# An attention stage's hand-written order: denominators ahead, all score blocks ahead of transposes, the next pair's preparation among the groups

## The chip, the cores and the metric

The kernel runs on one core of one Trainium2 chip. The metric is the device time of one execution in microseconds (us), and the time shown is a median of several executions. Work runs on five engines side by side, each of which takes its own instructions strictly in order: TensorE (PE: matmuls and transposes; its weight loads are listed as PEld), VectorE (DVE), ScalarE (ACT), GpSimd (POOL) and SyncE (SP, which here issues all DMAs). An instruction that waits for another engine holds up everything that stands behind it on its own engine.

## What is computed

Attention over 4 batches x 8 heads, 576 positions, head size 64, with a causal mask, mixed with a linear-attention memory; its output feeds two feed-forward blocks.

```python
scores = scale * np.matmul(q, k.transpose(0, 1, 3, 2))    # causal mask, softmax
local = np.matmul(a, v)
q_p = phi(q)                                              # elu(q) + 1
mem_out = einsum('bhsd,bhde->bhse', q_p, M_prev) / (einsum('bhsd,bhd->bhs', q_p, z_prev) + 1e-06)
out = g * mem_out + (1 - g) * local                       # g: one gate per head
...
h = x @ w_in;  x = (h * np.tanh(softplus(h))) @ w_out     # 2304 x 512, width 2048
x = (((x @ w1) * (x @ w2)) @ w3) @ w_out2                 # width 1024
```

## The kernel before

The attention stage takes two heads at a time: 16 pairs, each with all 576 positions. Function `pair(p)` writes out one pair's work, and it is software-pipelined over two pairs: `now` is pair p, whose scores are computed, `old` is pair q = p - 1, whose second half is finished, and `new` is pair p + 1, whose inputs are prepared. Pairs 1 to 15 are emitted under `tc.manual_schedule()`, so the order in which `pair` writes the steps sets the order on the engines; pair 0 and the trailing call for pair 15's rest are placed by a scheduler.

The steps, with the names that the rows below use:

- `s_blocks(p, e, blocks)`: scores of head e (0 or 1) of the pair for the row blocks given (block 3 is 128x512, block 2 128x384, blocks 1 and 0 share a bank), two matmuls each from `eqk` (head 0) or `oqk` (head 1) and `lk`,`qz` into a `psA` bank (three banks); then on DVE the masked negative maximum (L405, with a short read of the accumulator), then on ACT the exponential with its row sum (L410). `s_last(p)` does the same for the last 64 rows of both heads (`s4`, matmuls on `qd`).
- `inverted` (L391, L392) takes the reciprocal of the row sums, `normed` (L400) scales a block by it.
- `pt_g(p, i)`: transposes of one group of scaled blocks on PE into a `psF` bank (two banks), and one copy out on ACT (L470). Groups 0 to 2 are head 0, 3 to 5 head 1, 6 and 7 the last rows.
- `prep_q`, `prep_k`: PE transposes the raw q and k of the next pair into `psX` banks (three); ACT copies them out (`qt` L319, `hk` L330), POOL or DVE makes the low halves (`hl`, `lk`). `stack` then copies them by DMA into `eqk`, `oqk` and `qz`.
- `prep_phi(p)`: phi of the queries (ACT L366, POOL L367, DVE L368).
- `weigh_phi(q)`: the memory's denominators. PE multiplies phi by z (`zt`, five products of two columns, L59), DVE adds 1e-6 and inverts (`dn`, L380, L381), ACT spreads the ten values over 640 columns (`spread`, L384), PE transposes that (five transposes, L301), DVE multiplies phi by it (L387).
- `pv_main(q)`, `pv_last(q)`: one product of phi and the memory and the products of weights and values, in one `psX` bank; ACT copies out the high half (`xt`, L474), DVE makes the low half (L65).
- `background` is a generator that decodes weights for the next stage in single steps, seven for each weight tile: a 512 KB DMA into `draw` (L92, one buffer), DVE L99, L101, L103, L106, L108, L110, then POOL L111. `pair` takes seven of its steps in each of pairs 2 to 9, and the generator is empty after that.

After the attention stage come the two feed-forward blocks, which are a scheduler's work and are not touched.

Of the kernel before, what the change touches and what calls it, by code (L numbers as in the profile page):

```python
# [14 lines left out]
ALU = mybir.AluOpType  # L15
# [6 lines left out]
def fused_kernel(ctx: ExitStack, tc, q, k, v, M_prev, z_prev, beta, w_in, w_out, w1, w2, w3, w_out2, out):  # L22
    nc = tc.nc
# [271 lines left out]
    def trans(src, evac):  # L295
        for c0, c1 in ((0, 256), (256, S)):
            pt = psX()

            for i in range(2) if c0 == 0 else (2, 3, 4):
                x = min(128 * i, S - 128) - c0  # L300
                nc.tensor.transpose(pt[:, x:x + 128], src[:, i].rearrange("p h d -> p (h d)"), ident)  # L301
            evac(slice(c0, c1), pt[:, 0:c1 - c0])
# [65 lines left out]
        nc.vector.scalar_tensor_tensor(out=t, in0=t, scalar=1.0, in1=r, op0=ALU.min, op1=ALU.add)  # L368
        st[p]["phi"] = t

    def weigh_phi(p):
        b, c = divmod(p, NP)
        t = st[p]["phi"]

        o = psF()[:, 0:2 * NB]
        for i in range(NB):
            x = min(128 * i, S - 128)
            mm(o[:, 2 * i:2 * i + 2], t[:, x:x + 128], zt[b % 2][:, c], True, True)
        dn = ap_.tile([128, 2 * NB], F32, tag="dn", name="dn", bufs=2)
        nc.vector.tensor_scalar(out=dn, in0=o, scalar1=1e-6, scalar2=None, op0=ALU.add)  # L380
        nc.vector.reciprocal(out=dn, in_=dn)  # L381

        w = ap_.tile([128, NB, 2, D], F32, tag="spread", name="spread", bufs=1)
        nc.scalar.copy(  # L384
            out=w.rearrange("p i e d -> p (i e) d"), in_=dn[:, :, None].to_broadcast([128, 2 * NB, D]),
        )
        trans(w, lambda cs, o: nc.vector.tensor_tensor(out=t[:, cs], in0=o, in1=t[:, cs], op=ALU.mult))  # L387

    def inverted(p, e):
        rv = st[p]["sum"][:, slice(8, 9) if e is None else slice(e, 8, 2)]  # L390
        nc.vector.tensor_scalar(out=rv, in0=rv, scalar1=1e-9, scalar2=None, op0=ALU.add)  # L391
        nc.vector.reciprocal(out=rv, in_=rv)  # L392

    def normed(p, ib, e):

        d = st[p]
        og = ogp[:, p % NP]
        s = s4[:, 0:S] if ib == 4 else d["s"][ib, e]
        x = 8 if ib == 4 else 2 * ib + e
        nc.vector.tensor_scalar(  # L400
            out=s, in0=s, scalar1=d["sum"][:, x:x + 1], scalar2=og[:, x:x + 1], op0=ALU.mult, op1=ALU.mult
        )
# [58 lines left out]
    def pt_g(p, gi):  # L461
        d = st[p]
        n = 128 * len(GROUPS[gi])
        t = ap_.tile([128, n], F32, tag=f"pt{gi}", name="pt", bufs=1)
        o = psF()
        for x, (ib, e, jb) in enumerate(GROUPS[gi]):
            src = d["s"][4] if e is None else d["s"][ib, e]
            nc.tensor.transpose(o[:, 128 * x:128 * x + 128], src[:, 128 * jb:128 * jb + 128], ident)  # L468
            d["t"][ib, e, jb] = t[:, 128 * x:128 * x + 128] if e is None else (t, 128 * x)
        nc.scalar.copy(out=t, in_=o[:, 0:n])  # L470
# [82 lines left out]
    def pair(p):  # L553

        now, old, new = p < NPAIR, p > 0, p + 1 < NPAIR
        q = p - 1
        background = first if 2 <= p < 12 else iter(())
        if old:
            ensure_x(q // NP)
        if now and old:  # L560
            stack(p, 1)

        if old:
            inverted(q, 1)
            normed(q, 3, 1)
        if now:
            s_blocks(p, 0, (3,))
        if old:
            normed(q, 2, 1)
        if now:  # L570
            s_blocks(p, 0, (2,))
        if old:
            pt_g(q, 5)
            normed(q, 1, 1)
            normed(q, 0, 1)
        if now:
            s_blocks(p, 0, (0, 1))
        if old:
            pt_g(q, 4)
            pt_g(q, 3)  # L580
            inverted(q, None)
            normed(q, 4, None)
        if new:
            prep_q(p + 1)
        if old:
            pt_g(q, 6)
        if new:
            prep_k(p + 1)
        if old:
            pt_g(q, 7)  # L590
            weigh_phi(q)
        steps(background, 2)

        if now:
            if new:
                stack(p + 1, 0)
                last_q(p + 1)
            inverted(p, 0)
            normed(p, 3, 0)
            s_blocks(p, 1, (3,))  # L600
            normed(p, 2, 0)
            s_blocks(p, 1, (2,))
            normed(p, 1, 0)
            normed(p, 0, 0)
        if old:
            if not now:
                steps(lq0, 100)
                emit_h((0, 0, 0))
            pv_main(q)
        if now:  # L610
            s_blocks(p, 1, (0, 1))
            pt_g(p, 2)
            pt_g(p, 1)
            steps(background, 2)
            pt_g(p, 0)
        if old:
            pv_last(q)
        if now:
            s_last(p)
        steps(background, 2)  # L620
        if new:
            prep_phi(p + 1)
        if p + 2 < NPAIR:
            load_pair(p + 2)
        steps(background, 1)

    lq0 = first
    for p in range(NPAIR + 1):
# [219 lines left out]
```

## Time and profile before

| | |
|---|---|
| median of 2 runs | 1185.32 us (1185.30 and 1185.33) |
| profiled execution | 1186.9 us, of which the span from first to last instruction 1185.1 us |
| busy: PE, PEld | 1063.3 us (90%), 954.0 us (80%) |
| busy: DVE, ACT, POOL | 676.2 us (57%), 551.6 us (47%), 303.9 us (26%) |
| mean granted TensorE clock | 0.949 of full speed |

The profile was taken in one execution. Its own time lies 1.6 us above the median, and 1.8 us of it are outside the span. The busy shares are means over stages that have different limits: up to about 392 us the program is in the attention stage, where PE is busy between 60% and 80% of the time, and after that in matrix products that keep PE nearly full.

### The profile page before, as it was taken

Reading aid. Unit: us, or ns where it says so; the run is one execution under the profiler, and the core shown is the slowest. Engines: PE = TensorE matmul, PEld = TensorE weight load, DVE = VectorE, ACT = ScalarE, POOL = GpSimd, SP = SyncE. Lnnn points to the kernel's source line nnn. Section 1 sums busy time; section 2 is a strip of 40 time slices with the busy share of each in tenths; the row PEclk is TensorE's granted clock in tenths of the full one; section 3 lists DMA queues with packets and bytes.
Section 4 is the critical chain, followed back from the end, with each engine's and each line's share of the span. In section 5 each row is a group of like instructions: output and inputs, shape, how many; then the busy total and the mean of one; then the engine's idle time right before and its main releaser. Section 6 shows DMA issues by size and latency. Waiting matters only on the chain.

```text
span 1185.1 us, 19371 instructions
## 1 busy us (share of the span) xinstructions
PE 1063.3 (90%) x7288; PEld 954.0 (80%) x7288; DVE 676.2 (57%) x1643; ACT 551.6 (47%) x1159; POOL 303.9 (26%) x271
## 2 busy tenths in 40 slices
PE   6777677777778999999999999999999799999998
PEld 5646555555557899999999998999899599999997
DVE  5566756665555798898878875465564122222120
ACT  5545544555553765666655665455232122222221
POOL 5332352233110364555554450010110000000000
PEclk9888988888989999999999999999999899999999
DMA  6555555645522133333442237334121400000000
GB/s 154 122 133 135 123 130 125 135 91 119 126 56 72 55 116 116 125 92 123 132 133 91 90 129 280 125 125 142 61 68 51 169 28 18 18 11 9 19 19 36
DMA packets 111214, 115.68 MB, mean 98 GB/s; under 512 B 73616, under 2 KB 73616, under 8 KB 111120
## 3 DMA queue, kind: packets, MB, share of 16 engines
q1 hardware_dynamic: 111120, 114.44, 34.1%
q8 instruction: 58, 0.95, 0.3%
q14 instruction: 36, 0.29, 0.1%
HBM read 70.79 MB, written 21.50 MB: 78 GB/s over the span
## 4 chain that ended last, share of the span: by engine, by line
PE 55%; DVE 22%; ACT 7%; DMA 5%; POOL 5%; issue 4%; SPq 0%; DVEq 0%; POOLq 0%; ACTq 0%
PE psA L59 25%; PE psX L59 19%; PE psF L59 6%; DVE de L110 3%; ACT s L410 3%; DVE da L106 3%; PE psX L301 2%; DVE de L108 2%; DVE s L405 2%; DVE da L99 2%; PE psF L468 2%; ACT pt L470 2%; POOL da L139 2%; DVE da L101 2%; DVE da L103 2%
## 5 line engine op out<-in xcount | busy, mean ns | idle before, releaser
L111 POOL TENSOR_TENSOR da<-da,de 128x512 f32<-128x512 f32 x72 | 98.7, 1373 | 490.3 <-DVE de L110 388.1
L59 PE MATMUL psX<-gh,wqt 128*128 128x288 f32 x1024 | 210.7, 299 | 12.7 <-DVE x L669 7.0
L59 PE MATMUL psA<-x2h,w12t 128*128 128x256 f32 x1152 | 210.6, 283 | 0.2 <-ACT x2h L764 0.2
L59 PEld LDWEIGHTS psA<-x2h,w12t 128*128 128x128 f32 x1152 | 180.9, 192 | 1.8 <-ACT x2h L764 0.6
L59 PEld LDWEIGHTS psX<-gh,wqt 128*128 128x128 f32 x1024 | 164.9, 189 | 17.7 <-DVE x L669 9.4
L59 PE MATMUL psA<-x2l,w12t 128*128 128x256 f32 x576 | 163.2, 284 | 0.4 <-DVE x2l L65 0.4
L59 PE MATMUL psX<-gl,wqt 128*128 128x288 f32 x512 | 151.3, 296 | 1.1 <-DVE gl L65 1.1
L410 ACT ACTIVATE s<-s,acc 128x128 f32<-128x128 f32 (+3 forms) x144 | 83.5, 580 | 113.5 <-DVE acc L405 112.7
L778 DVE TENSOR_TENSOR bs<-bs,psA 128x256 f32<-128x256 f32 x72 | 30.3, 420 | 167.9 <-PE psA L59 167.7
L468 PE MATMUL psF<-ident,s 128*128 128x128 f32 x400 | 67.6, 291 | 60.7 <-ACT pt L470 37.2
L59 PE MATMUL psA<-xt,wqt 128*128 128x288 f32 x840 | 120.2, 296 | 1.3 <-DVE y L533 1.3
L59 PEld LDWEIGHTS psA<-xt,wqt 128*128 128x128 f32 x840 | 114.5, 188 | 2.0 <-DVE y L533 1.6
L59 PEld LDWEIGHTS psA<-x2l,w12t 128*128 128x128 f32 x576 | 110.5, 192 | 1.3 <-DVE x2l L65 0.7
L59 PE MATMUL psX<-wft,pbuf 128*128 128x512 f32 x432 | 102.2, 396 | 7.5 <-DMA wft<-w_dram 7.5
L468 PEld LDWEIGHTS psF<-ident,s 128*128 128x128 f32 x400 | 46.6, 147 | 76.8 <-ACT pt L470 46.4
L59 PEld LDWEIGHTS psX<-wft,pbuf 128*128 128x128 f32 x432 | 81.9, 191 | 25.4 <-DMA wft<-w_dram 8.7
L59 PEld LDWEIGHTS psX<-gl,wqt 128*128 128x128 f32 x512 | 96.8, 189 | 1.6 <-DVE gl L65 1.3
L779 ACT CAST pbuf<-bs 128x256 fp32r<-128x256 f32 x72 | 29.2, 406 | 109.0 <-DVE bs L778 95.5
L59 PE MATMUL psF<-xt,wqt 128*128 128x288 f32 x552 | 77.7, 295 | 0.4 <-DVE dn L380 0.3
L59 PEld LDWEIGHTS psF<-xt,wqt 128*128 128x128 f32 x552 | 74.5, 188 | 0.8 <-DVE dn L380 0.5
L99 DVE TENSOR_SCALAR da<-draw 128x512 int32<-128x512 int32 x72 | 40.7, 566 | 60.1 <-DMA draw<-in_moe_w_dram 16.2
L536 ACT CAST gh<-y 128x576 fp32r<-128x576 f32 x64 | 43.1, 674 | 66.9 <-DVE y L533 51.1
(117 smaller groups left out, 1959.4 us busy)
## 6 DMA issues: line engine op xcount, KB each, us to landing
draw<-in_moe_w_dram SPq DMA_DIRECT2D x32, 512.0 KB, 3.7
draw<-in_moe_w_out_dram SPq DMA_DIRECT2D x24, 512.0 KB, 3.6
draw<-in_moe_w_in_dram SPq DMA_DIRECT2D x16, 512.0 KB, 4.1
w12t<-w_dram SPq DMA_DIRECT2D x8, 1024.0 KB, 7.3
w_dram<-de SPq DMA_DIRECT2D x24, 256.0 KB, 2.1
w_dram<-da SPq DMA_DIRECT2D x24, 256.0 KB, 2.1
out_dram<-ob SPq DMA_DIRECT2D x18, 256.0 KB, 2.0
eqk<-hk SPq DMA_DIRECT2D x30, 144.0 KB, 2.5
```

Source lines behind the costliest of these rows:

```text
L59: nc.tensor.matmul(o, lhsT=l, rhs=r, start=start, stop=stop)
L99: V.tensor_scalar(out=ai, in0=hw, scalar1=0x7FFFFFFF, scalar2=None, op0=ALU.bitwise_and)
L101: V.tensor_scalar(out=a, in0=a, scalar1=2.0 ** -15, scalar2=122879.9921875, op0=ALU.max, op1=ALU.min)
L103: V.tensor_scalar(out=ai, in0=ai, scalar1=3, scalar2=0x3FFFFFF8, op0=ALU.logical_shift_left, op1=ALU.bitwise_and)
L106: V.scalar_tensor_tensor(out=ai, in0=hw, scalar=-0x40000000, in1=ai, op0=ALU.bitwise_and, op1=ALU.bitwise_or)
L110: V.scalar_tensor_tensor(out=e, in0=lw.bitcast(U32), scalar=2.0 ** -52, in1=e, op0=ALU.mult, op1=ALU.mult)
L111: nc.gpsimd.tensor_tensor(out=a, in0=a, in1=e, op=ALU.add)
L410: nc.scalar.activation(out=s, in_=s, func=AF.Exp, scale=-1.0, bias=a, accum_out=r)
L468: nc.tensor.transpose(o[:, 128 * x:128 * x + 128], src[:, 128 * jb:128 * jb + 128], ident)
L536: nc.scalar.copy(out=gh, in_=y[i])
L778: nc.vector.tensor_tensor(out=bs, in0=bs, in1=pa, op=ALU.mult)
L779: nc.scalar.copy(out=t[:, 0, m], in_=bs)
```

## The change

It touches the order in `pair`, and cuts `weigh_phi` into three steps that can stand apart: `norm_phi` (the products with z, the addition and the reciprocal on DVE), `spread_phi` (the copy on ACT) and `weigh_phi` (the transposes and the multiplication). No instruction is added or removed; each has the same operands and sizes as before.

- `norm_phi(q)` now stands first in a pair, ahead of the first score block.
- All three score steps of head 0 stand ahead of group 5's transposes, with `spread_phi` between block 2 and blocks 0 and 1. All three of head 1 stand ahead of `pv_main`.
- `prep_q` stands before group 5, `prep_k` before groups 4 and 3, and `weigh_phi` between group 3 and group 6.
- `pt_g(p, 0)` moves behind `pv_last`, and the last steps of `background` are taken together (2 + 2 + 3 in place of 2 + 2 + 2 + 1).

```diff
--- before.py
+++ after.py
@@ -368,7 +368,7 @@
         nc.vector.scalar_tensor_tensor(out=t, in0=t, scalar=1.0, in1=r, op0=ALU.min, op1=ALU.add)
         st[p]["phi"] = t
 
-    def weigh_phi(p):
+    def norm_phi(p):
         b, c = divmod(p, NP)
         t = st[p]["phi"]
 
@@ -379,12 +379,19 @@
         dn = ap_.tile([128, 2 * NB], F32, tag="dn", name="dn", bufs=2)
         nc.vector.tensor_scalar(out=dn, in0=o, scalar1=1e-6, scalar2=None, op0=ALU.add)
         nc.vector.reciprocal(out=dn, in_=dn)
-
+        st[p]["dn"] = dn
+
+    def spread_phi(p):
         w = ap_.tile([128, NB, 2, D], F32, tag="spread", name="spread", bufs=1)
         nc.scalar.copy(
-            out=w.rearrange("p i e d -> p (i e) d"), in_=dn[:, :, None].to_broadcast([128, 2 * NB, D]),
+            out=w.rearrange("p i e d -> p (i e) d"),
+            in_=st[p]["dn"][:, :, None].to_broadcast([128, 2 * NB, D]),
         )
-        trans(w, lambda cs, o: nc.vector.tensor_tensor(out=t[:, cs], in0=o, in1=t[:, cs], op=ALU.mult))
+        st[p]["w"] = w
+
+    def weigh_phi(p):
+        t = st[p]["phi"]
+        trans(st[p]["w"], lambda cs, o: nc.vector.tensor_tensor(out=t[:, cs], in0=o, in1=t[:, cs], op=ALU.mult))
 
     def inverted(p, e):
         rv = st[p]["sum"][:, slice(8, 9) if e is None else slice(e, 8, 2)]
@@ -561,6 +568,7 @@
             stack(p, 1)
 
         if old:
+            norm_phi(q)
             inverted(q, 1)
             normed(q, 3, 1)
         if now:
@@ -570,25 +578,26 @@
         if now:
             s_blocks(p, 0, (2,))
         if old:
-            pt_g(q, 5)
-            normed(q, 1, 1)
-            normed(q, 0, 1)
+            spread_phi(q)
         if now:
             s_blocks(p, 0, (0, 1))
         if old:
-            pt_g(q, 4)
-            pt_g(q, 3)
+            normed(q, 1, 1)
+            normed(q, 0, 1)
+        if new:
+            prep_q(p + 1)
+        if old:
+            pt_g(q, 5)
             inverted(q, None)
             normed(q, 4, None)
         if new:
-            prep_q(p + 1)
-        if old:
-            pt_g(q, 6)
-        if new:
             prep_k(p + 1)
         if old:
+            pt_g(q, 4)
+            pt_g(q, 3)
+            weigh_phi(q)
+            pt_g(q, 6)
             pt_g(q, 7)
-            weigh_phi(q)
         steps(background, 2)
 
         if now:
@@ -601,6 +610,7 @@
             normed(p, 2, 0)
             s_blocks(p, 1, (2,))
             normed(p, 1, 0)
+            s_blocks(p, 1, (0, 1))
             normed(p, 0, 0)
         if old:
             if not now:
@@ -608,21 +618,19 @@
                 emit_h((0, 0, 0))
             pv_main(q)
         if now:
-            s_blocks(p, 1, (0, 1))
             pt_g(p, 2)
             pt_g(p, 1)
             steps(background, 2)
-            pt_g(p, 0)
         if old:
             pv_last(q)
         if now:
+            pt_g(p, 0)
             s_last(p)
-        steps(background, 2)
         if new:
             prep_phi(p + 1)
         if p + 2 < NPAIR:
             load_pair(p + 2)
-        steps(background, 1)
+        steps(background, 3)
 
     lq0 = first
     for p in range(NPAIR + 1):
```

PE's own order at the head of a pair, before; `hk,qd` is the end of the pair ahead (`s_last`), the numbered `s` are blocks that `pt_g` transposes:

```order
L59 MATMUL psA<-hk,qd 128x288 x2
L59 MATMUL psA<-lk,qd 128x288
L59 MATMUL psA<-eqk 128x512
L59 MATMUL psA<-lk,qz 128x512
L59 MATMUL psA<-eqk 128x384
L59 MATMUL psA<-lk,qz 128x384
L468 MATMUL psF<-ident,s_1214 128x128
L468 MATMUL psF<-ident,s_1207 128x128
L59 MATMUL psA<-eqk 128x256
```

The same place now:

```order
L59 MATMUL psA<-hk,qd 128x288 x2
L59 MATMUL psA<-lk,qd 128x288
L59 MATMUL psF<-zt_115,phi 128x2 x5
L59 MATMUL psA<-eqk 128x512
L59 MATMUL psA<-lk,qz 128x512
L59 MATMUL psA<-eqk 128x384
L59 MATMUL psA<-lk,qz 128x384
L59 MATMUL psA<-eqk 128x256
L59 MATMUL psA<-lk,qz 128x256
L59 MATMUL psA<-eqk 128x256
L59 MATMUL psA<-lk,qz 128x256
L301 MATMUL psX<-ident,raw 128x128 x5
```

The five products with z stand ahead of the first score block, and group 5 no longer stands ahead of blocks 0 and 1.

PE in the middle of a pair, before, from the products with z to the second half of head 1's scores:

```order
L59 MATMUL psF<-zt_115,phi 128x2 x5
L301 MATMUL psX<-ident,spread 128x128 x5
L59 MATMUL psA<-oqk 128x512
L59 MATMUL psA<-lk,qz 128x512
L59 MATMUL psA<-oqk 128x384
L59 MATMUL psA<-lk,qz 128x384
L59 MATMUL psX<-phi,mr_111 128x512
L59 MATMUL psX<-pt,raw 64x512 x2
L59 MATMUL psX<-pt,raw 64x384 x2
L59 MATMUL psX<-pt,raw 64x256 x2
L59 MATMUL psX<-pt,raw 64x128 x2
L59 MATMUL psA<-oqk 128x256
```

The same place now (`s_121` is the last rows' block, groups 6 and 7):

```order
L301 MATMUL psX<-ident,spread 128x128 x5
L475 MATMUL psF<-ident,s_121 128x128 x5
L59 MATMUL psA<-oqk 128x512
L59 MATMUL psA<-lk,qz 128x512
L59 MATMUL psA<-oqk 128x384
L59 MATMUL psA<-lk,qz 128x384
L59 MATMUL psA<-oqk 128x256
L59 MATMUL psA<-lk,qz 128x256
L59 MATMUL psA<-oqk 128x256
L59 MATMUL psA<-lk,qz 128x256
L59 MATMUL psX<-phi,mr_111 128x512
```

The products with z are gone from here, groups 6 and 7 stand behind the spread's transposes, and all of head 1's scores stand ahead of `pv_main`.

DVE between the first readers of a `draw` tile and the next, before; behind these rows follow the two multiplications of phi (L387) and then L99 on the next tile:

```order
L110 SCALAR_TENSOR_TENSOR de<-draw,de 128x512
L405 ISA s_1596,acc<-psA,mask 128x128
L405 ISA acc 128x1
L405 ISA s_1599,acc<-psA,mask 128x256
L405 ISA acc 128x1
L391 TENSOR_SCALAR sum<-sum 128x1
L392 RECIPROCAL sum<-sum 128x1
L400 TENSOR_SCALAR s_121<-s_121,sum,ogp 128x576
L65 TENSOR_TENSOR lk<-psX,hk 128x256
L65 TENSOR_TENSOR lk<-psX,hk 128x320
L380 TENSOR_SCALAR dn<-psF 128x10
L381 RECIPROCAL dn<-dn 128x10
```

The same place now:

```order
L108 TENSOR_SCALAR de<-da 128x512
L399 RECIPROCAL sum<-sum 128x1
L110 SCALAR_TENSOR_TENSOR de<-draw,de 128x512
L407 TENSOR_SCALAR s_121<-s_121,sum,ogp 128x576
L65 TENSOR_TENSOR lk<-psX,hk 128x256
L65 TENSOR_TENSOR lk<-psX,hk 128x320
L394 TENSOR_TENSOR phi<-psX,phi 128x256
L394 TENSOR_TENSOR phi<-psX,phi 128x320
L99 TENSOR_SCALAR da<-draw 128x512
```

The last reader of one tile (L110) stands behind the score blocks' maxima instead of ahead of them, so five instructions are left between it and the first reader of the next tile.

## Rows read from the trace of the kernel before

**Rows 1.** Stages: busy us of each engine, granted clock, cut where `pv_main` begins.

```profile
core 0: us, PE busy (x) PEld busy (x) DVE busy (x) ACT busy (x) POOL busy (x), PEclk, DMA share, GB/s
39.41:60.51 21.10, 16.24 (x113) 12.11 (x113) 12.42 (x46) 12.09 (x34) 5.46 (x5) 0.90 0.66 149
60.51:249.74 189.23, 139.30 (x897) 102.81 (x897) 124.26 (x400) 97.99 (x272) 66.93 (x59) 0.85 0.56 126
249.74:360.26 110.52, 85.72 (x552) 61.53 (x552) 61.90 (x219) 59.40 (x166) 20.21 (x17) 0.86 0.45 96
395.00:1185.00 790.00, 762.31 (x5375) 728.68 (x5374) 439.86 (x863) 343.69 (x594) 186.65 (x156) 0.99 0.26 89
```

**Rows 2.** The chain that ended last, in order of time: start, us, what.

```profile
126.17 1.29 PE psF L59 x10
...
163.22 1.24 PE psA L59 x7
...
172.58 1.87 PE psF L59 x10
...
174.47 0.18 DVE dn L380
...
174.68 0.23 DVE dn L381
...
174.98 0.73 ACT spread L384
...
175.76 1.33 PE psX L301 x5
...
178.59 3.91 PE psX L59 x18
...
182.52 0.60 ACT xt L474
...
183.14 0.69 DVE xt L65
...
185.06 0.26 ACT pt L470
185.32 0.04 issue
185.36 0.66 PE psF L468 x4
...
186.92 1.25 PE psA L59 x7
```

**Rows 3.** Timeline of DVE in the same pair: start, us, instruction, [idle before, releaser].

```profile
164.91 0.69 DVE L106 SCALAR_TENSOR_TENSOR da<-draw,da 128x512 int32<-128x512 int32 x1
...
167.32 0.67 DVE L400 TENSOR_SCALAR s<-s,sum,ogp 128x256 f32<-128x256 f32 x2
...
168.57 0.69 DVE L110 SCALAR_TENSOR_TENSOR de<-draw,de 128x512 f32<-128x512 uint32 x1
...
169.72 0.15 DVE L391 TENSOR_SCALAR sum<-sum 128x1 f32<-128x1 f32 x1
...
170.11 0.81 DVE L400 TENSOR_SCALAR s<-s,sum,ogp 128x576 f32<-128x576 f32 x1
172.83 0.82 DVE L65 TENSOR_TENSOR lk<-psX,hk 128x256 fp32r<-128x256 f32 x2 [1.91 <-ACT hk L330]
...
177.97 0.15 DVE L391 TENSOR_SCALAR sum<-sum 128x4 f32<-128x4 f32 x1
...
178.83 0.68 DVE L405 CUSTOM_DVE_ANT_0 s<-psA,mask 128x512 f32<-128x512 f32 x1
```

**Rows 4.** The `draw` tile's instructions: its DMAs' time from issue to landing.

```profile
DMA to landing us min/median/max: 3.5/3.9/4.4
```

**Rows 5.** ACT's lines from 60.51 to 249.74 us: busy, mean ns | idle before.

```profile
L410 ACT ACTIVATE s<-s,acc 128x512 f32<-128x512 f32 (+4 forms) x72 | 41.8, 581 | 63.8 <-DVE acc L405 63.4
L470 ACT COPY pt<-psF 128x512 f32<-128x512 f32 (+1 forms) x64 | 29.9, 492 | 3.5 <-PE psF L468 3.5
L330 ACT CAST hk<-psX 128x256 fp32r<-128x256 f32 (+1 forms) x16 | 5.8, 435 | 0.0
L319 ACT COPY qt<-psX 128x256 f32<-128x256 f32 (+1 forms) x16 | 5.6, 409 | 0.0
```

**Rows 6.** The granted clock (0.51 is 1.2 GHz) in one pair, columns as in rows 1.

```profile
166.00:172.90 6.90, 4.34 (x32) 3.48 (x32) 4.92 (x18) 5.53 (x17) 3.39 (x4) 1.00 0.26 83
172.90:179.90 7.00, 5.68 (x20) 4.21 (x19) 4.27 (x14) 1.46 (x4) 4.71 (x4) 0.51 0.77 166
```

**Rows 7.** Timeline of PE in that pair, where it sat idle.

```profile
166.74 0.41 PE L468 MATMUL psF<-ident,s 128*128 128x128 f32 x2 [1.72 <-DVE s L400]
...
171.07 0.63 PE L468 MATMUL psF<-ident,s 128*128 128x128 f32 x4 [1.41 <-ACT pt L470]
```

## The prediction

> **What bounds the kernel now.** I read the stages first. After 395 us PE is busy 762 of 790 us at a clock of 0.99 [rows 1]; nothing is moved there, so that part stays. Before it stand the pairs of heads, and there no engine is full: in the eight pairs that decode weights a pair takes 189.23 / 8 = 23.65 us, with DVE busy 15.5, PE 17.4 and ACT 12.2; in the six without decoding (21.10 + 110.52) / 6 = 21.94 us, with DVE 12.4 and PE 17.0 [rows 1]. A pair is bound by waits that pass from engine to engine, so I took the chain next. In its middle stands a stretch in single file [rows 2]: PE's products with z (1.87 us at half clock, 1.29 in the pair ahead), DVE's addition and reciprocal (0.18, 0.23), ACT's spread (0.73), the spread's transposes (1.33). DVE then multiplies phi, decodes L99, and comes to the sums of head 0 only at 177.97 [rows 3]. A second single file stands at the end: `pv_main` (3.91, with the phi-memory product), ACT's copy of it (0.60), DVE's low half (0.69), and only then the maximum of blocks 0 and 1 of head 1, their exponentials, group copies, group 0's transposes (0.66) and `s_last` [rows 2].
>
> **The change, laid out over one pair.** A pair runs from one `s_last` to the next: 163.22 to 186.92, 23.70 us [rows 2]. I cut it at two places on DVE: the last maximum of head 0 (169.72) and the start of head 0's sums (177.97) [rows 3]. The three parts now take 6.50, 8.25 and 8.95 us.
>
> *Part one, decoding pair.* New at its head are the products with z, on PE behind `s_last`. The row of 1.24 us holds `s_last`'s six products and one more [rows 2], so about 0.9 for the six; with 1.29 the products are done at 2.2 us. DVE is free of `s_last`'s maxima at 164.91 - 163.22 = 1.7 [rows 3], so it waits 0.5: that is the price of a wait that did not stand there. Behind it on DVE stand the sums and scalings of head 1 and head 0's maxima; PE's score blocks stand behind the products too, but are done before DVE gets to them. Then DVE has the addition and reciprocal, 174.47 to 174.9, 0.44 [rows 2]; sum, reciprocal and scaling of block 3, 177.97 to 178.83, 0.86 [rows 3]; and what it has today between 164.91 and 169.72, 4.81, without the two scalings (0.58, from 167.32 to 167.90) and L110 (0.60, from 168.57 to 169.17), which move behind the maxima: 3.63. The part ends at 2.23 + 0.44 + 0.86 + 3.63 = 7.2 us, 0.7 later than today. That group 5's transposes no longer stand ahead of blocks 0 and 1 takes away PE's wait of 1.72 us for a scaled block [rows 7], but I cost it at nothing in this part: DVE had work all that time.
>
> *Part two.* The scalings, sum and reciprocal (0.39, 169.72 to 170.11) and L110 come to 7.2 + 0.58 + 0.39 + 0.60 = 8.7 us. Then the last rows' scaling (0.81), the two subtractions for `lk` (0.82) [rows 3], and the two multiplications of phi, of the same shapes as `lk`'s: 0.82. That makes 11.2 us. DVE's wait of 1.91 for `hk` [rows 3] goes: ACT now copies q and k out behind one short group copy, where two long ones and then a third stood, about 2.5 x 0.49 us less [rows 5], and DVE comes 1.2 us later by the moved scalings and L110; the spread, 0.73 ahead of the last exponentials on ACT, takes back part. The multiplication waits for nothing new, since the spread lies ready and its transposes stand in PE's queue behind group 3. What is late next is a DMA. L110 is the last reader of a `draw` tile, L99 the first of the next, there is one buffer, and a load lands 3.9 us after issue [rows 4]: at 8.7 + 0.05 + 3.9 = 12.7. Today L110 and L99 stand 8 us or more apart and it is hidden; now DVE stands 1.5 us at L99, with all of head 1's first half queued behind. With some 0.4 for L99 the part ends at 13.1, 5.9 us where it takes 8.25.
>
> *Part three.* Sum, reciprocal, scaling 0.86, maximum of block 3 about 0.6: 14.6 us. Head 1's scores are on PE by then, all three of them, so ACT's four exponentials run without a break: 4 x 0.58 = 2.3 [rows 5], 16.9 us. `pv_main` starts on PE near 12.3 (phi is ready at 11.2, then the scores) and at 3.9 us [rows 2] ends at 16.2, under the exponentials. Then ACT's copy of it 0.6, group 2's short copy 0.4 (under the mean of 0.49, rows 5, since it is half as wide), which group 0 waits for as a `psF` bank, and group 0's transposes 0.66 [rows 2]: `s_last` at 18.6, 5.5 us where it takes 8.95. DVE's low half and the maximum and exponentials of blocks 0 and 1 no longer stand between `pv_main` and group 0; that is most of the gain. `pv_last`, moved ahead of group 0, runs while PE would wait for that copy.
>
> A **decoding pair** at full clock is thus 18.6 us. A pair **without decoding** lacks L106, L108, L110, L99 and the wait for `draw`; ACT sets it. Maximum of block 3 at 4.1; exponentials and spread, 2.3 + 0.73, to 7.1; copies of q 0.82, group 5 0.4, k 0.87 [rows 5] to 9.2; the second subtraction and the second half of the spread's transposes to about 10.1; groups 6 and 7 about 0.8, scores about 1.5 (1.6 times `s_last`'s columns), `pv_main` 3.3 to 3.9 to about 16; copies and group 0, 1.66, to 17.6 us.
>
> **The clock** is not in that. Today the granted clock falls to 1.2 GHz once in the pair shown, for 7.0 us (0.51 there, 1.00 ahead of it) [rows 6], after PE had stood idle 1.72 and 1.41 us and shorter times between [rows 7]. After the change PE still stands: its second transposes of k wait for the copy of q, about 2.5 us. So I keep one such fall a pair. It would lie over transposes, scores and `pv_main`, about 5.5 us of PE work, and lengthen them by 2 to 3 us at most; PE has 0.7 to spare against ACT in part three. I take 1.5 us in a decoding pair and 1.2 in the others: **20.1 and 18.8 us**.
>
> POOL and SP keep their work. `hl` comes on POOL at about 9 us, with one L111 (waiting for L110) between its two halves in some pairs; `eqk` would then land near 16 and is needed after 20. SP issues some loads of v ahead of the last copies into `oqk` and `qz`, which are needed half a pair later. Both at nothing; if that cover were gone, PE's first score block would wait.
>
> **The sum.** 8 x (23.65 - 20.1) + 6 x (21.94 - 18.8) = 28.4 + 18.8 = 47 us. The profiled execution took 1186.9 us and the median is 1185.3; set against the median, 1138 us. Ends: with no clock loss (18.6 and 17.6) 8 x 5.05 + 6 x 4.34 = 66 us, 1119; with the full 3 us (21.6 and 20.6) 24 us, 1161. Pair 0, pair 1's head and the trailing call I leave as they are.
>
> **Rivals.** *New waits take back half.* ACT's queue now holds the spread and four exponentials ahead of the copies of q, PE's transposes of k and groups 4 and 3 wait for those, and DVE waits for `draw`; if each costs about 1 us beyond the layout, the pairs take 21.5 to 22.5 and 20.5 to 21.5, which is 1150 to 1175. For it: a single file is easily longer than its pieces. Against: the layout already has DVE and ACT waiting there.
>
> *The clock stays low, and the kernel is slower.* PE's idle time gathers into one stretch behind the scores; if the clock stayed at 1.2 GHz for most of each pair, PE would bind. Its 17.4 us of busy time at a mean clock of 0.85 are about 14.5 at full clock; below a mean of 14.5 / 23.65, about 0.6, its own work fills today's pair, and at 0.5 a pair is up to 27 us (less, since not all of it scales): 26 is 8 x 2.4 + 6 x 4 = 43 us slower, 1228. Against: today's idle stretches are as many, and the clock comes back within 7 us [rows 6].
> The Trainium skill, page "TensorE: Matmul & The Clock Gate", section "Loop structure matters more than you think", says that the loop nest decides whether matmuls keep the full clock, and that a long wait between bursts of them costs it. By that rule the fall of rows 6 behind the idle stretches of rows 7 is what to expect, the trace agrees, and gathering the idle time would speak against this change.
>
> *More than forecast.* The fall of the clock goes with the idle time, or L99 finds its tile there: 1105 to 1122.
>
> *The order does nothing*, because DVE's and ACT's work was the bound anyway: 1185. Against: DVE is busy 15.5 of 23.65 us.
>
> **How the numbers follow.** Forecast (1122 to 1150) 0.58, half taken back 0.24, more 0.10, nothing 0.04, slower 0.04. A measurement tells about 2% from no change, 24 us, so faster means below 1161.6: forecast, more, and over half of the second case, 0.81; slower 0.04; the same 0.15. The range 1116 to 1164 leaves out the top third of the second case, the last two and the far end of the best.
>
> **What would show it.** Pairs of about 20 and 19 us between one `pv_main` and the next; no idle time of DVE ahead of `dn` in the middle and about half a microsecond at the head; L99 waiting 1 to 2 us for the DMA into `draw`; `xt` waited for by DVE about 1 us, where ACT's exponentials stand ahead of it; PE's clock near 0.85. Wrong would be a mean clock near 0.7, DVE idle over 5 us a pair, or ACT's copies of q starting after 9 us in the pair.

## The result and the profile after

The changed kernel takes 1134.72 us (median; 1131.41 to 1138.02) where the kernel before takes 1185.32: a ratio of 0.957, 95% interval 0.945 to 0.969, 50.6 us faster. The forecast was 1138. The profiled execution took 1138.02 us, 1136.2 of them span, so 48.9 us of span are to be accounted for. Cut into the stages of [rows 1], with the columns named there, the trace of after says:

```profile
37.10:54.78 17.68, 14.95 (x115) 12.19 (x113) 12.14 (x43) 12.58 (x34) 3.66 (x5) 0.90 0.73 165
54.78:232.00 177.22, 132.11 (x898) 106.30 (x897) 122.24 (x402) 98.39 (x272) 63.46 (x54) 0.86 0.63 134
232.00:319.65 87.65, 74.18 (x552) 59.68 (x551) 64.51 (x222) 61.08 (x166) 27.55 (x23) 0.90 0.59 127
```

Against [rows 1], from one `pv_main` to the next:

| stretch | before | after | gain | forecast |
|---|---|---|---|---|
| up to the first `pv_main` | 39.4 | 37.1 | 2.3 | 0 |
| six intervals without decoding | 21.10 + 110.52 | 17.68 + 87.65 | 26.3 | 18.8 |
| eight intervals with decoding | 189.23 | 177.22 | 12.0 | 28.4 |
| last interval, into the trailing call (360.26 to 385.13; 319.65 to 337.00) | 24.87 | 17.35 | 7.5 | 0 |
| all that follows | 800.0 | 799.2 | 0.8 | 0 |
| sum | | | 48.9 | 47.2 |

The total is as forecast, the terms are not. The term that was to bring most brought less than half, and three others made it up. An engineer who had compared only the totals would have missed that.

The eight decoding pairs are also uneven, which those of before are not (22.9 to 24.4 us): 19.05, 24.44, 24.71, 19.67, 24.47, 20.90, 27.07, 16.91. Three of them, in the same view:

```profile
73.83:98.27 24.44, 19.79 (x114) 16.80 (x113) 15.03 (x50) 12.36 (x34) 8.09 (x7) 0.72 0.59 121
167.12:188.02 20.90, 14.15 (x115) 10.83 (x113) 14.83 (x50) 12.01 (x34) 7.43 (x7) 1.00 0.59 134
215.09:232.00 16.91, 13.93 (x114) 10.82 (x113) 14.53 (x50) 12.49 (x34) 2.43 (x3) 1.00 0.67 142
```

DVE and ACT are busy for nearly the same time in each of the three; what differs is how long they stand, and the clock. So the waits come next. DVE's waits in the kernel before, from 40 to 350 us (engine, tile and line that wait, what released them: us in total, times, longest):

```profile
DVE xt L65 <- ACT xt L474: 48.3, 28, 3.3
DVE lk L65 <- ACT hk L330: 25.8, 13, 2.1
DVE phi L387 <- PE psX L301: 22.6, 24, 1.6
DVE dn L380 <- PE psF L59: 5.9, 13, 1.0
```

and in the changed kernel:

```profile
DVE da L99 <- POOL wqt L65: 29.1, 7, 6.0
DVE xt L65 <- ACT xt L481: 21.3, 22, 2.2
DVE phi L394 <- PE psX L301: 9.7, 14, 1.4
DVE lk L65 <- ACT hk L330: 4.9, 7, 0.7
DVE dn L380 <- PE psF L59: 4.8, 11, 1.4
```

Of the eight decoding intervals alone (55 to 232 us) the same view, PE's weight loads with DVE, has these, to which the later parts come back:

```profile
DVE da L99 <- POOL wqt L65: 28.1, 6, 6.0
PEld psX L301 <- ACT qt L319: 21.5, 8, 3.8
DVE xt L65 <- ACT xt L481: 8.2, 8, 1.3
DVE dn L380 <- PE psF L59: 3.1, 5, 1.4
```

The four waits that the change was to shorten (`xt`, `lk`, `phi`, `dn`) fall from 102.6 to 40.7 us; the window is the same for both kernels and leaves out the last 35 us of the pairs of before. A new one of 29.1 us, nearly all of it in the eight, stands at L99, and it is for POOL, not for the DMA into `draw` that the prediction expected there. L99 writes `da`, which has one buffer, and POOL's subtraction of `da` (`wqt`, L65) is its last reader. POOL's timeline around the `pv_main` at 98.27, where the first of the three rows above ends, shows why it is late (start, us, instruction, [idle before, releaser]):

```profile
93.39 0.83 POOL L62 TENSOR_SCALAR hl<-qt 128x576 fp32r<-128x576 f32 x1 [16.35 <-ACT qt L319]
94.19 1.46 POOL L111 TENSOR_TENSOR da<-da,de 128x512 f32<-128x512 f32 x1
95.62 1.40 POOL L65 TENSOR_TENSOR hl<-qt,hl 128x576 fp32r<-128x576 f32 x1
97.00 0.61 POOL L62 TENSOR_SCALAR wqt<-da 128x512 fp32r<-128x512 f32 x1
97.58 0.74 POOL L339 TENSOR_TENSOR qd<-hl,own 128x256 fp32r<-128x256 f32 x1
98.29 2.13 POOL L367 TENSOR_SCALAR relu<-qt 128x576 f32<-128x576 f32 x1
100.38 1.26 POOL L65 TENSOR_TENSOR wqt<-da,wqt 128x512 fp32r<-128x512 f32 x1
```

and DVE's at the same place what that costs:

```profile
96.19 0.49 DVE L394 TENSOR_TENSOR phi<-psX,phi 128x320 f32<-128x320 f32 x1 [0.22 <-PE psX L301]
101.68 0.43 DVE L99 TENSOR_SCALAR da<-draw 128x512 int32<-128x512 int32 x1 [5.00 <-POOL wqt L65]
```

The preparation of q now comes early in the pair, so `hl`, `qd` and `relu` get into POOL's queue between the decoding's own steps. In the kernel before, POOL's timeline has the decoding's three steps in one piece, done at 172.75, while L99 came only at 177.54 (the instruction ahead of the sums in [rows 3]): 4.8 us of slack. Over the seven tiles from 60 to 250 us that slack is 3.5 to 5.0 us, and L99 waits there for nothing.

```profile
169.34 1.26 POOL L111 TENSOR_TENSOR da<-da,de 128x512 f32<-128x512 f32 x1 [14.26 <-DVE de L110]
170.69 0.71 POOL L62 TENSOR_SCALAR wqt<-da 128x512 fp32r<-128x512 f32 x1
171.48 1.27 POOL L65 TENSOR_TENSOR wqt<-da,wqt 128x512 fp32r<-128x512 f32 x1
```

In the eight, L99 stands 5.33, 5.00, 6.02, 4.62 and 5.79 us (it starts at 77.08, 101.68, 147.09, 170.60 and 192.68), and 1.33 us at 123.18. The five long waits fall into the five longest intervals, 20.90 to 27.07 us; the other three take 16.91 to 19.67.

DVE's stand reaches TensorE. PE's row behind it, and the clock on both sides (columns as in rows 1):

```profile
104.13 1.89 PE L475 MATMUL psF<-ident,s 128*128 128x128 f32 x6 [2.53 <-DVE s L407]
```

```profile
98.27:103.70 5.43, 3.33 (x20) 1.25 (x18) 1.95 (x7) 0.08 (x1) 3.38 (x3) 1.00 1.21 204
103.70:110.40 6.70, 6.13 (x42) 5.56 (x42) 4.22 (x16) 4.34 (x13) 0.00 (x0) 0.51 0.83 165
```

PE stands 2.53 us for a scaled block that DVE delivers late, and the next 6.7 us run at 1.2 GHz. The two intervals at a clock of 1.00 take 16.91 and 20.90 us, the two at 0.91 take 19.05 and 19.67, and the four at 0.72 to 0.81 take 24.44 to 27.07.

### The profile page after: what moved, and what is told of

It is laid out like the page before. It is cut to its first block, busy times and chain, and to the rows that moved or that the text cites. A ratio compares the mean times of both kernels' runs of the same rounds, so it can differ in the third digit from the quotient of the medians.

```text
span 1136.2 us, 19376 instructions
## 1 busy us (share of the span) xinstructions
PE 1040.5 (92%) x7288; PEld 956.9 (84%) x7288; DVE 674.1 (59%) x1643; ACT 554.2 (49%) x1159; POOL 306.2 (27%) x271
## 4 chain that ended last, share of the span: by engine, by line
PE 54%; DVE 22%; POOL 9%; DMA 5%; issue 5%; ACT 4%; SPq 0%; ACTq 0%; DVEq 0%; POOLq 0%
PE psA L59 25%; PE psX L59 18%; PE psF L59 6%; PE psF L475 4%; DVE de L110 3%; DVE da L106 2%; DVE s L407 2%; DVE da L99 2%; POOL da L111 2%; PE psX L301 2%; DVE s L412 2%; DVE de L108 2%; POOL wqt L65 2%; ACT s L417 2%; DVE da L101 2%
## 5 line engine op out<-in xcount | busy, mean ns | idle before, releaser
L59 PE MATMUL psX<-gh,wqt 128*128 128x288 f32 x1024 | 212.2, 301 | 10.8 <-DVE x L677 6.6
L111 POOL TENSOR_TENSOR da<-da,de 128x512 f32<-128x512 f32 x72 | 100.2, 1395 | 390.7 <-DVE de L110 270.7
L475 PE MATMUL psF<-ident,s 128*128 128x128 f32 x400 | 77.4, 334 | 29.9 <-DVE s L407 28.2
L99 DVE TENSOR_SCALAR da<-draw 128x512 int32<-128x512 int32 x72 | 39.3, 550 | 90.4 <-POOL wqt L65 40.8
L475 PEld LDWEIGHTS psF<-ident,s 128*128 128x128 f32 x400 | 58.0, 172 | 39.3 <-issue 32.1
L477 ACT COPY pt<-psF 128x512 f32<-128x512 f32 (+2 forms) x128 | 60.2, 493 | 31.7 <-PE psF L475 30.3
```

Source lines behind the costliest of these rows:

```text
L59: nc.tensor.matmul(o, lhsT=l, rhs=r, start=start, stop=stop)
L99: V.tensor_scalar(out=ai, in0=hw, scalar1=0x7FFFFFFF, scalar2=None, op0=ALU.bitwise_and)
L111: nc.gpsimd.tensor_tensor(out=a, in0=a, in1=e, op=ALU.add)
```

## The experiments

My theory was that the loss in the decoding pairs is POOL's late release of `da` (theory A where an expectation uses the letter). The first rival: L99 is only the place where a lateness shows, and with POOL out of the way DVE would stand there for the load, or elsewhere for as long. Runs 1 to 4 and 9 tell these apart. Of the rest of the gain the theory was that each of the three rearrangements (denominators, head 1's scores, preparation) brings a share that its undoing takes away again, against one of them bringing all of it; runs 5 to 8, 11 and 12 are for that. The times below are medians, each against the kernel before as it ran beside it; "the eight" and "the five" are the eight decoding intervals and the last five without decoding between `pv_main`s, from the profile.

**1. The sum goes into the other buffer.** In attention's decoding POOL writes the sum of L111 into `de` in place of `da`, so that `da` is free behind L111 and `wqt` reads `de`.

```diff
-    def decoder(stack, raw, n):
...
+    def decoder(stack, raw, n, into_de=False):
...
+        if dec["into_de"]:
+            nc.gpsimd.tensor_tensor(out=e, in0=a, in1=e, op=ALU.add)
+            return e, a
         nc.gpsimd.tensor_tensor(out=a, in0=a, in1=e, op=ALU.add)
         return a, e
...
-    decoder(at, 1, 1)
+    decoder(at, 1, 1, True)
```

> The changed kernel, but in the attention stage the decode's last addition on POOL writes the sum into the tile de in place of da, so da is free when that addition ends and no longer only after the rounding and the subtraction behind it. Same instructions. Theory A (DVE's L99 stands in the changed kernel because POOL holds da until its last subtraction, which is queued behind the halves of q, qd and relu: six waits of 28.1 us in eight pairs): L99 waits 0 to 2 us, then for the draw load; the eight decoding pairs go from 22.15 us to about 20, 15 to 20 us in all, about 1117 us. Rival B (my prediction's step: the single draw buffer's load, 3.9 us, sets L99): nothing changes, 1132 to 1138 us. Rival C (the decode's own DVE and POOL work sets these pairs): nothing changes either, but L99 shows no wait for the load.

1123.12 us, ratio 0.9465 (0.9446 to 0.9484); the eight take 161.69 us, 20.2 each, where the changed kernel takes 22.2. The waits of the eight at L99:

```profile
DVE da L99 <- DMA draw<-in_moe_w_in_dram: 9.6, 4, 2.8
DVE da L99 <- DMA draw<-in_moe_w_out_dram: 6.6, 4, 2.5
```

POOL's hold is gone and the load shows: 16.2 us in eight waits, 2.0 each. The prediction had 1.5 there, and 20.1 us for the pair. So POOL's hold was a cost of its own, 15.5 us in the eight, as the theory has it, and behind it stands the load, as the rival has it, which POOL had hidden.

**2. L99 later.** The decoding's steps are dealt out otherwise: one before head 1, three behind group 1, so that L99 comes behind DVE's low half.

```diff
-        steps(background, 2)
+        steps(background, 1)
...
             pt_g(p, 1)
-            steps(background, 2)
+            steps(background, 3)
```

> The changed kernel with one number moved: L99 of the next weight tile is taken with L101 and L103, behind head 1's maxima, and no longer ahead of head 0's sums. POOL's queue then has both last steps of the decode ahead of the next halves of q, and the load has 4 us more. Theory A: no wait at L99, decoding pairs 19 to 20 us, 17 to 25 us less in all, 1110 to 1118 us. Rival B: the same move hides the load too, 12 us less at most (8 x 1.5), 1120 to 1125. Rival C: 1132 to 1138.

1104.68 us, 0.9312 (0.9295 to 0.9329), 82 us faster than the kernel before beside it, and the fastest of all kernels here. The eight together, columns as in rows 1:

```profile
53.73:199.17 145.44, 119.33 (x899) 95.16 (x898) 136.54 (x406) 98.36 (x272) 67.77 (x55) 0.93 0.78 164
```

18.2 us a pair, at a clock of 0.93 in place of 0.86; the eight gain 31.8 us on the changed kernel, more than the 17 to 25 that the theory gave. POOL's order has not mended: its `wqt` of one pair still ends at 112.2. But DVE has other work until then, and L99 follows it without a wait (in the eight it waits once, 0.7 us):

```profile
112.18 0.68 DVE L65 TENSOR_TENSOR xt<-psX,xt 128x512 fp32r<-128x512 f32 x1
112.78 0.41 DVE L99 TENSOR_SCALAR da<-draw 128x512 int32<-128x512 int32 x1
```

This removes POOL's hold and the load's wait together, so it can't tell the two apart; beside run 1 it says that L99 in its early place costs 32 us, of which run 1 gives back 15.5.

**3. Both edits.**

> Both edits together. Theory A: the first is superfluous when L99 stands late; within 3 us of the late L99 alone. If the wait for da is still in part there in the second kernel, this one is faster by 5 us or more.

1117.34 us, between 1105.85 and 1123.63 from one execution to the next; 0.9384 (0.9331 to 0.9437) against run 2's 0.9312 (0.9295 to 0.9329). It is not better than run 2, so beside a late L99 the first edit adds nothing, as the theory has it. But the theory's "within 3 us" is missed by the median, 12.7 us above run 2, while one execution of the four is as fast as run 2. Why the executions lie so far apart is not shown.

**4. The other buffer in the kernel before.** The edit of run 1, made to the kernel before.

> The kernel before with the decode's last addition into de. In the trace of before L99 waited for nothing in the pairs, as POOL was done with da long before. Theory A: no change, 1183 to 1188 us. Rival (da's release held the pairs before the change as well): 10 us or more less.

1186.09 us, 0.9993 (0.9978 to 1.0009); the eight take 189.25 against 189.23. Where L99 has 3.5 to 5.0 us of slack, freeing `da` earlier is worth nothing. The edit of run 1 has no merit of its own; it pays only for the hold that the new order made.

**5. Denominators back between group 3 and group 6.** All else as changed.

```diff
-            norm_phi(q)
             inverted(q, 1)
...
-            spread_phi(q)
...
             pt_g(q, 3)
+            norm_phi(q)
+            spread_phi(q)
             weigh_phi(q)
```

> The changed kernel with one part undone: the products with z, the reciprocal, the spread and the weighing of phi stand in one piece again, behind group 3. My layout: products 1.29, addition and reciprocal 0.44, spread 0.73 with gaps come back in single file, less the 0.5 us of wait that they cost at the head: pairs without decoding 17.5 to about 19.5 us; decoding pairs less than that, as L99 then comes later and waits less for POOL: 0 to 1 us more. 1144 to 1156 us. Rival (this part hid behind ACT's copies anyway, and only the order of the score blocks counts): no change, within 4 us of the changed kernel.

1154.77 us, 0.9722 (0.9705 to 0.9738), 16 us slower than the changed kernel beside it (1138.57, run 8). The five take 100.45 (20.1 each against 17.8), the last interval 22.25 against 17.35. Its waits from 40 to 350 us, with the columns as above:

```profile
ACT spread L386 <- DVE dn L381: 30.2, 15, 2.4
DVE phi L394 <- PE psX L301: 25.3, 28, 1.6
DVE dn L380 <- PE psF L59: 23.6, 13, 2.4
DVE da L99 <- POOL wqt L65: 15.0, 7, 3.1
```

The single file of [rows 2] is back in three rows, and is worth 2.3 us a pair. The eight, however, take 170.77, 6.8 less than in run 8: DVE comes to L99 later, and POOL's hold falls from 27.5 us (run 8, same stretch) to 15.0. Of run 8's 27.5 the view puts 21.8 down to POOL and one wait of 5.7 down to a DMA, but that L99 begins at 144.12 and POOL's subtraction for `wqt` ends at 144.09.

**6. Blocks 0 and 1 of head 1 back behind `pv_main`.**

```diff
-            s_blocks(p, 1, (0, 1))
             normed(p, 0, 0)
...
             pv_main(q)
         if now:
+            s_blocks(p, 1, (0, 1))
             pt_g(p, 2)
```

> The changed kernel with one part undone: blocks 0 and 1 of head 1 stand behind pv_main again. My layout: DVE's low half 0.7, a maximum and two exponentials, about 2.5 us in all, stand between pv_main and group 0 again: pairs without decoding 17.5 to about 20, decoding pairs about 2 us more, 14 pairs: 1160 to 1172 us. Rival (ACT's four exponentials set part three, whatever stands ahead of pv_main): 0.5 us a pair or less, 1134 to 1142.

1149.26 us, 0.9683 (0.9652 to 0.9713), 11 us slower than run 8. The five take 88.26, as changed (88.94), but at a clock of 0.96 where run 8 has 0.88. Interval by interval they are some 0.7 us longer at a like clock: 17.18 and 17.19 us against 16.51 at 1.00, 18.65 and 18.77 at 0.91 against 17.68 and 18.02 at 0.90 and 0.91. The loss in time is in the eight, 187.69 against 177.59, in intervals of 22.3 and 25.5 us and then of 18 to 19 and 27 to 29 by turns, at a mean clock of 0.79. The chain of waits through one long interval (start, us, what) runs through POOL's queue into L99, and from there through DVE's low half into the last exponentials:

```profile
74.06 2.10 POOL relu L367
76.17 1.25 POOL wqt L65
...
77.44 0.43 DVE da L99
...
80.96 0.48 ACT xt L481
...
81.46 0.69 DVE xt L65
...
82.39 0.37 ACT s L417
```

Where DVE is late by POOL's hold, the low half stands behind that in single file, and the part that the change moved away from there is worth something. L99 itself waits no longer than in run 8: four long waits, 20.5 us in all, one in each of the four longest intervals. That the low half is what makes the rest of the loss is read from the chain; whether the edit of run 2 makes the loss go away was not tried. Without decoding the moved part is worth some 0.7 us a pair in this surrounding, and the higher clock takes that back.

**7. Preparation back behind groups 4 and 3.** `prep_q` behind the last rows' scaling, `prep_k` behind group 6, `weigh_phi` behind group 7, as before; denominators and scores as changed.

```diff
-        if new:
-            prep_q(p + 1)
         if old:
             pt_g(q, 5)
+            pt_g(q, 4)
+            pt_g(q, 3)
...
         if new:
+            prep_q(p + 1)
+        if old:
+            pt_g(q, 6)
+        if new:
             prep_k(p + 1)
         if old:
-            pt_g(q, 4)
-            pt_g(q, 3)
+            pt_g(q, 7)
             weigh_phi(q)
-            pt_g(q, 6)
-            pt_g(q, 7)
```

> The changed kernel with one part undone: the preparation of the next pair's q and k and the weighing of phi stand where they stood before the change, q behind groups 5 to 3, k behind group 6, the weighing behind group 7. My layout gave this part about 1.2 us a pair (copies of k behind one short group copy instead of three): pairs without decoding about 18.5. In decoding pairs the halves of q come later on POOL; theory A: POOL holds da as long or longer, so these pairs gain nothing. 1140 to 1155 us. Rival (the preparation's place is worth nothing): 1132 to 1138.

1131.52 us, 0.9527 (0.9509 to 0.9544), 7 us *faster* than run 8. The eight take 164.52 against 177.59, the five 90.81 against 88.94. From 40 to 350 us:

```profile
DVE lk L65 <- ACT hk L330: 36.2, 16, 3.9
DVE da L99 <- POOL wqt L65: 2.8, 2, 1.7
```

The wait for `hk` that the early preparation had removed is back (4.9 us in after), and POOL's hold is almost gone; in the eight L99 waits 1.7 us for POOL and 0.3 for the load. In the decoding pairs the cure was dearer than the ill.

**8. The changed kernel beside runs 5 to 7.**

> The changed kernel itself on the chip of these runs, as the base that they are compared with: 1131 to 1138 us, decoding pairs with long waits at L99 behind POOL (several of 5 us), their number differing from execution to execution.

1138.57 us, 0.9589 (0.9564 to 0.9613); the eight 177.59, the five 88.94, the last interval 17.35.

**9. Late L99, and the preparation back.** Runs 2 and 7 together: if the early preparation is bad in itself, this is faster than run 2; if it hurts only by POOL's hold, slower.

> The kernel with the late L99 and, in it, the preparation of q and k and the weighing undone as in e7. In e7 undoing this part made the kernel faster by 7 us, by 13 us less in the decoding pairs and 2 us more in the five without decoding. Theory A: the part hurts only because it brings POOL's halves of q ahead of the decode's last subtraction; where L99 stands late that no longer matters, and undoing the part then costs what it costs in pairs without decoding or more, 0.4 to 1.5 us a pair: 1109 to 1125 us, against 1104.7 for the late L99 with the part. Rival (the preparation among the groups is worth nothing or less, with or without that wait): 1100 to 1107 us.

1121.99 us, 0.9473 (0.9451 to 0.9495), 17 us slower than run 2; the eight take 156.72 against 145.44. Without the hold the early preparation is worth 11 us in the eight; with it, it costs 13 (runs 7 and 8). What made the early preparation bad was the wait at L99: POOL's hold, with the load behind it, since the late L99 takes both away. Beside run 7, where L99 waits only 2.0 us in the eight, the late L99 still gives 7.8 us (164.52 to 156.72), so run 2's 32 us need not all be that wait.

**10. Late L99, and the spread behind `prep_k`.** Does ACT's spread (0.54 to 0.73 us) ahead of the last exponentials still cost?

```diff
             s_blocks(p, 0, (2,))
-        if old:
-            spread_phi(q)
...
             prep_k(p + 1)
         if old:
+            spread_phi(q)
             pt_g(q, 4)
```

> The kernel with the late L99, and ACT's spread moved behind the copies of k. In it PE still waits 2.3 us a pair for ACT's copy of q, which stands behind the spread (0.7 us). If that wait is on the chain, pairs get 0.3 to 0.7 us shorter: 1095 to 1101 us. If the chain runs elsewhere (SP's copies into oqk, which POOL's halves of q wait for), no change: 1102 to 1107.

1110.15 us (1105.67 to 1115.73), 0.9386 (0.9352 to 0.9419): no gain over run 2. The place that the change gave the spread is not what is left to win.

**11 and 12. One part alone, in the kernel before.** In run 11 only the denominators move: the products with z first, the spread ahead of group 5, `weigh_phi` where it was. In run 12 only blocks 0 and 1 of head 1 move ahead of `pv_main`.

```diff
         if old:
+            norm_phi(q)
             inverted(q, 1)
...
         if old:
+            spread_phi(q)
             pt_g(q, 5)
```

> The kernel before with one part of the change alone: products with z and reciprocal at the head of a pair, spread ahead of group 5, weighing where it stood. Undoing this part in the changed kernel (e5) cost 16 us: 2.3 us in a pair without decoding. If the parts add up, alone it gives the same: pairs without decoding 22.1 to about 19.8, decoding pairs 23.65 to about 21.5, 1145 to 1160 us. If it pays only together with the preparation among the groups (copies of k then end the middle), alone it gives under 1 us a pair: 1172 to 1185.

1168.04 us (1163.44 to 1170.76), 0.9845 (0.9811 to 0.9878), 19 us faster than before.

```diff
             normed(p, 1, 0)
+            s_blocks(p, 1, (0, 1))
             normed(p, 0, 0)
...
             pv_main(q)
         if now:
-            s_blocks(p, 1, (0, 1))
```

> The kernel before with one part of the change alone: all of head 1's score blocks ahead of pv_main. Undoing it in the changed kernel (e6) cost nothing in pairs without decoding, against the 2.5 us of my layout. In the chain of before DVE's low half, a maximum and two exponentials (0.69 + 0.2 + 0.8 us) stand between pv_main and the group copies. If that stretch is worth its length there, pairs get 1.2 to 1.7 us shorter: 1160 to 1170 us. If ACT's four exponentials take its place at once, as e6 says, under 0.5 us a pair: 1178 to 1187.

1176.35 us (1171.24 to 1177.12), 0.9898 (0.9864 to 0.9931), 11 us faster than before. Runs 11 and 12 are each within 2% of the kernel before, but with the interval clear of 1. In runs 6, 7, 11 and 12, as in run 10, the time fell into neither of the ranges that stood in the expectation: that each part has a share of its own is too simple, and so is that one of them brings all of it.

Together, in us (a kernel with a part undone keeps the smaller edits, among them head 0's order and group 0 behind `pv_last`; one with a part alone lacks them, so the table is no pure sum of parts):

| what is in place | the five | the eight | clock in the eight |
|---|---|---|---|
| nothing (before) | 110.5 | 189.2 | 0.85 |
| denominators (11) | 100.7 | 190.1 | 0.78 |
| scores (12) | 99.8 | 191.2 | 0.75 |
| scores and preparation (5) | 100.5 | 170.8 | 0.82 |
| denominators and preparation (6) | 88.3 | 187.7 | 0.79 |
| denominators and scores (7) | 90.8 | 164.5 | 0.85 |
| all (after) | 87.7 | 177.2 | 0.86 |
| all, and L99 late (2) | 89.7 | 145.4 | 0.93 |

In the five, denominators or scores alone bring 10 us, denominators with either of the other two bring 20 to 22, and the third adds 3 at most. Scores and preparation stand in for one another there, as far as these runs show (the preparation alone was not tried); the denominators have no stand-in. The clock of the five is 0.84 to 0.91 in all rows but the one of run 6, 0.96. In the eight, one part alone brings nothing, and its clock falls below that of before. Among these runs the gain there comes with the scores and one more part, and most of it an L99 that doesn't wait.

## Why the prediction was right, and where it was wrong

**What bounds the kernel: right.** It is waits from engine to engine. No instruction was taken away, and the four waits of DVE that the layout named fall by 62 us.

**The step that failed: "What is late next is a DMA", and POOL "at nothing".** The layout asked which wait L99 would meet in its earlier place, and looked at one of its two operands: the `draw` tile that it reads. The `da` tile that it writes has one buffer too, and its last reader stands on POOL. The prediction did see that POOL would get `hl` at about 9 us "with one L111 (waiting for L110) between its two halves in some pairs", but priced only what that does to `eqk`, and left out `qd`, `relu` and the two `wqt` steps, and who waits for them. In place of 1.5 us a pair at L99 the trace has 28.1 us in the eight (3.5 each), so 16 us more than priced; the decoding term came out 16.4 us short (12.0 in place of 28.4).

Run 1, which takes POOL's hold away and nothing else, gives 20.2 us a pair where the layout had 20.1, so with this one wait taken out the decoding pairs take as long as laid out in the mean (18.6 to 23.1 one by one). Its parts do so less well: one pair of run 1, cut as the prediction cuts it (at 143.89, 150.50, 157.69 and 163.89), has 6.6, 7.2 and 6.2 us at a clock of 1.00, where the layout at full clock had 7.2, 5.9 and 5.5; 2.49 of the 7.2 are the wait for the load. So that the mean comes out is in part luck. The chance of a loss at L99 was in "new waits take back half", as a DVE wait for `draw`, which is the wrong mechanism.

**Part one: right in size.** DVE's wait for the products with z is 3.1 us in the eight, 0.4 a pair (0.5 forecast). What the denominators are worth, 2.3 us a pair without decoding by run 5, the prediction did not price by itself.

**Part two: `lk` right, `draw` a little short.** The wait for `hk` falls from 25.8 to 4.9 us. The load's wait, once POOL no longer hides it, is 2.0 us against 1.5 (run 1). PE's stand behind ACT's copies of q, laid out at about 2.5 us, is 21.5 us in the eight, 2.7 each.

**Part three: about right in size, its reason only in part.** The prediction laid out a gain of 3.45 us in a decoding pair's last part (8.95 to 5.5; 6.2 in the pair of run 1) and called the low half and the maximum and exponentials that no longer stand between `pv_main` and group 0 "most of the gain". Putting them back (run 6) costs the five nothing, or 0.7 us a pair at a like clock. In the kernel before the same edit alone is worth 10.8 us in the five (run 12): it is a gain that the early preparation can also bring, so it may be counted once. In the eight, undoing it costs 10 us, 1.3 a pair. DVE's wait for ACT's copy of `xt`, forecast at about 1 us, is 8.2 us in the eight, 1.0 a pair.

**Pairs without decoding: 17.55 us where 18.8 was forecast** (105.33 / 6). Two of the six are at a clock of 1.00 and take 16.51 and 16.73 us, where the layout had 17.6, so the layout was about 1 us too long; the mean clock of 0.90 costs about as much again, near the 1.2 us laid aside for it. The chain of after in one of them shows the order laid out, with the reciprocal first, ACT's exponentials, spread and copies of q in a row, and then PE:

```profile
256.19 0.18 DVE dn L380
256.39 0.22 DVE dn L381
...
258.94 0.71 ACT s L417 x2
259.64 0.54 ACT spread L386
...
260.47 0.68 ACT s L417 x3
261.14 0.26 ACT qt L319
...
261.45 0.90 PE psX L301 x3
262.35 1.71 PE psF L475 x8
```

**The ends: left "as they are", and they gave 9.8 us.** Pair 1 and pair 15 are written out in the same order, so their halves gain too, and the trailing call has nothing beside it to cover the single file. Run 5 gives back 4.9 of the 7.5 us of the last interval by the denominators alone.

**The clock: right in the mean.** 0.86 in the eight where about 0.85 was expected. One like fall in each pair, as laid out, did not come: two intervals have none, and four stand at 0.72 to 0.81, among them the one shown above, with its fall at PE's stand. The rival in which it stays low did not come, though the runs with one part alone went that way (0.78 and 0.75 in the eight).

**So the total was right by compensation**: 16.4 us too much in one term, 7.5 and 9.8 too little in two others. Nothing in the layout made them cancel; that they did was luck. One of its rivals was also added up wrongly: pairs of 21.5 and 20.5 us make 1160 us by the prediction's own sum, not 1150.

**What stays open.** Why the denominators or the scores alone lower the clock in the decoding pairs so far that nothing is left of what they bring in the others. Whether the loss of run 6 in the eight goes away with a late L99. Why run 3 is no better than run 2. And some 1.6 us a pair of the 4.3 gained without decoding are in no part's undoing (2.3 for the denominators, 0.4 for the preparation, nothing for the scores, or 0.7 at a like clock): the order of head 0's scores and the move of group 0 were not undone by themselves, and parts that stand in for one another can't be told by undoing one.

## What to carry to other kernels

When an instruction is moved earlier, list everything that it waits for, the buffer that it writes as well as the data that it reads, and lay out the queue of each engine that has to let go of them, also of an engine that is never the bound: here POOL, busy 27% of the span, cost 16 us of the gain by the order of seven instructions. Where such a wait can't be shortened, moving the waiter behind work that has to be done anyway (run 2) was worth twice as much in the eight as freeing its buffer (run 1). And check a forecast stage by stage: a total that is right to some 3 us held a term that was wrong by 16.

## What the runs showed that I had not expected

- The granted clock in the eight decoding pairs goes from 0.75 to 0.93 with the order alone, PE's instructions being the same; PE's busy time there goes from 150.4 us (run 12) to 119.3 (run 2). In the pair shown above the stand of 2.53 us is followed by 6.7 us at half clock, so there PE loses time at the stand and again in the work behind it.
- The parts don't add up: two that alone bring 19 and 11 us come, with the third and the smaller edits, to 49, although undoing the third makes the kernel 7 us faster.
